# Block-sparse attention and a soft mixture of experts: the dense products joined, the slot input's vector steps moved

## The chip, the cores and the metric

The kernel runs on one core of one Trainium2 chip. A core has five engines with instruction queues of their own: TensorE (PE in the profile; its weight loads are listed apart as PEld), VectorE (DVE), ScalarE (ACT), GpSimd (POOL) and SyncE (SP, which here issues all DMAs). They meet through semaphores. SBUF is the memory that the engines work in, with 128 partitions; PSUM is the memory that PE writes its results to.

The metric is the device time of one execution in microseconds (us), taken as the median of several runs. A profile is one execution with every instruction recorded; its span is the time from the first to the last recorded instruction.

## The reference

Two stages, all in float32. First, block-sparse attention for 4 batches, 8 heads, 768 positions and head size 64, in 24 blocks of 32 positions:

```python
scores = scale * np.matmul(q, k.transpose(0, 1, 3, 2))
mask = np.abs(blk_i - blk_j) <= window          # window = 1: own block and both neighbours
mask = mask | (blk_i == 0) | (blk_j == 0) | (blk_i == n_blocks - 1) | (blk_j == n_blocks - 1)
for qb in range(n_blocks):
    for kb in sampled_blocks[qb]:               # 3 sampled blocks per query block
        mask[qb * block:(qb + 1) * block, kb * block:(kb + 1) * block] = True
scores = np.where(mask, scores, -1000000000.0)
attn = softmax(scores)                          # with 1e-9 added to the sum
out = np.matmul(attn, v)
```

So the first and the last query block see all 24 key blocks ("dense"), the other 22 see at most eight blocks of 32 ("sparse" or "band"). The heads side by side give x with 3072 rows of 512. Second, the mixture:

```python
logits = x @ phi                                # 32 slots: 8 experts with 4 slots each
d = softmax(logits, axis=0)                     # over all 3072 rows
slot_input = d.T @ x                            # 32 x 512
for e in range(8):                              # 4 slots each
    slot_out[e] = np.maximum(slot_input[e] @ w1[e], 0.0) @ w2[e]
c = softmax(logits, axis=1)                     # over the 32 slots
return c @ slot_out
```

w1 and w2 together are 32 MB (8 x 512 x 1024 floats twice).

## The kernel before

**Units.** Attention goes batch by batch. The eight heads are handled at once: four pairs on four groups of 32 partitions, and two halves r of the heads (r = 0, 1). A unit is one softmax step. A dense unit has one half r of the heads and one of the two dense query blocks j, with scores of 128 x 768; four of these make a batch's dense part. A sparse unit has one half r and a pair of neighbouring query blocks (number g of 11), with scores of 128 x 512. `ORDER0` and `ORDER` give the order in which dense (D) and sparse (S) units mix at the start of a batch: DDSSDDSS for the first batch, DSSDDDSS for the others, and then the sparse ones that are left.

**The main loop** (L617 to L677) makes one step n per unit. For each unit it issues, spread over several steps: staging of keys (`stage_k`: POOL and ACT copy the band's keys and the sampled blocks into `kst`, and SP loads queries), staging of gathered values (`stage_v`: POOL, into `vrs`), the scores on PE two units ahead (`do_qk`, into the PSUM tag `s` with 3 buffers), the maximum on DVE and the exponential on ACT (`do_soft`), the transposes of the probabilities on DVE (`do_tr`), and one step later the products with the values on PE. For the band these are `av_half` for a query tile of four query blocks, once per half r (48 and 40 records of one call appear in the timeline as `avt<-vrs` and `avt<-v,ptt`). For the dense blocks it is `av_dense`, once per half r, each with 24 key blocks and two groups g of 64 partitions. All go to `avt`, four PSUM banks in two sets of two, which tiles use in turn. `av_out` divides by the sum and writes x.

**The slot input.** Each finished tile (b, t) of 128 rows of x runs through `moe_front`, six steps e1 to e5: e1 transposes x on PE (`mxt`, in the single PSUM buffer of the tag `pt`) and copies it to `xT` on DVE; e2 makes logits on PE (line L484, into spare columns of `avt`), copied to `lp` by ACT; e3 sums and transposes them on PE (L491, L492, `mlt`, tag `pt` again), and DVE takes a running maximum (`top`, L474 and L477); e3b takes the exponential on ACT (`dT`, L499), a rescaling factor (`al`) and a copy of the logits (`lst`, L504); e4 transposes dT on PE (`md`, L508, tag `pt`), and DVE copies it to `d` (L329) and updates the sum (L512); e5 multiplies d with x on PE (L523, spare columns of `avt`) and DVE adds the result to `sacc` (L526). `EOFF` says in which step after the tile's last unit each of these is issued, and in which of the three lists of a step it stands: lists 0 and 1 at the start of a step (functions that they return run later in the step, after the transposes), list 2 at its end. So the pair (4, 2) is the end of the fourth step. `EOFFL` does the same for one late tile.

**What sets the order.** In the main loop PE and DVE run their instructions in the order in which the program emits them, by hand (`MAN`, manual schedule); after the loop ACT does too. POOL, SP, and ACT in the loop are ordered by the framework's planner, which places an instruction where its estimate finds it ready; a DMA emitted late can therefore stand early in SP's queue.

**Weights.** The 32 MB are loaded in 64 tiles of 512 KB. `NPRE` tiles have space of their own from the start. Two groups go into places that attention has finished with (`EARLYW`: one keys' buffer and the values' buffer v0, issued in the last batch), two more into the other keys' buffer and v1 (`LATEW`), and eleven (`lwb`) into the space of attention's own buffers, behind the loop. What is left goes into tiles that the experts have used up. Then the expert stage and the output follow.

Of the kernel before, what the change touches and what calls it, by code (L numbers as in the profile page):

```python
# [21 lines left out]
P = 128  # L22
# [13 lines left out]
NKST, NVR, NQ, NPTD = 4, 6, 3, 1  # L36
# [9 lines left out]
EOFF = [(2, 2), (4, 1), (4, 2), (4, 2), (5, 1), (6, 2)]  # L46
EOFFL = [(2, 2), (3, 1), (3, 2), (3, 2), (4, 1), (5, 0)]
# [8 lines left out]
NPRE, NLB = 13, 11  # L56
# [10 lines left out]
def attn_moe_kernel(ctx, tc, qT, kT, vtab, sampled, phi, w1, w2, out):  # L67
# [97 lines left out]
    ptd = [pst.tile([P, NB, 2, BLK], F32, name=f"ptd{r}") for r in range(NPTD)]  # L165
# [13 lines left out]
    def load_v(b):  # L179
        vb = vbuf[b % 2].rearrange("p (a f) -> p a f", a=2)  # L180
        if b < 2:
            for p in range(NP):
                POOL.memset(vb[32 * p:32 * p + 32, 1 - p % 2, :], 0.0)  # L183
        for p in range(NP):
            SP.dma_start(out=vb[32 * p:32 * p + 32, p % 2, :], in_=vtab[b, 32 * p:32 * p + 32, :])
        vtile[b] = vb.rearrange("p a (k r d) -> p a k r d", k=NBZ, r=2)
# [145 lines left out]
    def do_tr(u):  # L332
        if u.dense:
            if u.j == 0:
                ptn[0] += 1
            u.pt = ptd[ptn[0] % NPTD]
            for n in range(2):
                DVE.transpose(out=u.pt[:, 12 * n:12 * n + 12, u.j, :], in_=u.p[n])  # L338
        else:
            t, n = (u.g + 1) // 2, 2 * (u.g > 0 and u.g % 2 == 0)  # L340
            if n == 0:
                pts[u.b, t, u.r] = pw.tile([P, 8, 4, BLK], F32, tag="ptt", name="ptt", bufs=PTB)
            u.pt = pts[u.b, t, u.r]
            DVE.transpose(out=u.pt[:, :, n:n + 2, :].rearrange("p k j q -> p j k q"), in_=u.p.rearrange("p j (k q) -> p j k q", k=8))  # L344

    pts = {}
    ptn = [0]

# [14 lines left out]
    def av_out(b, t, av, lo, hi, rs_=slice(0, 2)):  # L363
        n = rs_.stop - rs_.start
        a = av[lo:hi, :, 0:4 * D1].rearrange("p g (r a d) -> p g r a d", r=2, a=2)[:, :, rs_]
        x = new_x(b, t).rearrange("p (g r a d) -> p g r a d", g=2, r=2, a=2)[lo:hi, :, rs_]
# [14 lines left out]
    def av_dense(u):  # L381
        vt = vtile[u.b]
        av = new_set((u.b, "d"), u.r)
        for k in range(NB):
            for g in range(2):
                s_ = slice(64 * g, 64 * g + 64)
                av_mm(av, 64, 64, g, u.r, u.pt[s_, k].rearrange("p j q -> p (j q)"), vt[s_, :, k, u.r, :],
                      k == 0, k == NB - 1)
        return (lambda: av_out(u.b, 0, av, 64, 128)) if u.r else None
# [38 lines left out]
    def moe_front(b, t):  # L428
# [60 lines left out]
        def e3():  # L489
# [3 lines left out]
            top(ps, ps[:, P:P + NS])  # L493
# [12 lines left out]
        def e4():  # L506
            ps = psA.tile([P, NS], F32, tag="pt", bufs=1, name="md")
            PE.transpose(ps, st["dT"][0:NS, :], ident[0:NS, 0:NS])  # L508
            st["d"] = pw.tile([P, NS], F32, tag="d", name="d", bufs=1)
            evac(st["d"], ps, "A" if (b, t) == (B - 1, NT - 2) else "D")  # L510
# [9 lines left out]
        def e5():  # L520
# [4 lines left out]
            if "al" in st:  # L525
                DVE.scalar_tensor_tensor(out=sacc, in0=sacc, scalar=st["al"], in1=ps,  # L526
                                         op0=ALU.mult, op1=ALU.add)
            else:
                DVE.tensor_copy(out=sacc, in_=ps)

        return [f1, f2, f3, e3b, e4, e5] if (b, t) == (B - 1, NT - 1) else [e1, e2, e3, e3b, e4, e5]
# [84 lines left out]
    vn = [0]  # L616
    for n in range(-3, N):  # L617
        if n >= 0:
            pump_k(n + KSTEP)
        while vn[0] < min(N, n + VSTEP + 1):  # L620
# [21 lines left out]
        if n >= 0:  # L642
            t = None
            if u.dense:
                if u.j == 1:
                    at(n + 1, 0, lambda u=u: av_dense(u))
                    t = 0 if u.r == 1 else None
# [12 lines left out]
            if t is not None:  # L660
                if t == 0:
                    both[u.b] = both.get(u.b, 0) + 1
                if n < N - 1 and (t > 0 or both[u.b] == 2):
                    fr = {}
                    for j in range(6):
# [58 lines left out]
    e[5]()  # L724
    c4[3] = c_split(3)
# [41 lines left out]
    load_group(LATEW[0])  # L767
# [205 lines left out]
```

## Time and profile before

| what | value |
|---|---|
| median of 3 runs | 458.24 us (455.7 to 458.44) |
| profiled execution | 453.23 us, of which the span is 451.5 us |
| PE busy | 355.6 us (79%) |
| DVE busy | 241.8 us (54%) |
| ACT busy | 187.4 us (42%) |
| POOL busy | 176.2 us (39%) |
| first dense product starts | 23.9 us |
| attention ends, last weights start to load | about 380 us |
| last weight tiles arrive | about 430 us |

A row of the timeline reads: start in us, duration in us, engine, line of the kernel, operation, out<-in with their shape, number of instructions (x), and in brackets the idle time of the engine just before and what ended it. Shapes such as 64*32 of PE are rows times columns of the array that an instruction uses; a float32 product leaves two records. A row of the table of windows reads: the window, its length, then busy time and instructions of PE, PEld, DVE, ACT and POOL in turn, the clock granted to PE (1.00 is full), the DMA engines' share and their GB/s. A row of a wait reads: who waited, for whom, total us, times, longest.

### The profile page before, as it was taken

How to read it: one execution, taken by the hardware profiler on the slowest of the kernel's cores; microseconds unless marked ns; L12 is line 12 of the kernel's file. 1: busy time of each engine (PE TensorE's matmuls, PEld its weight loads, DVE VectorE, ACT ScalarE, POOL GpSimd, SP SyncE). 2: the span in 40 equal slices, each digit the busy share in tenths (PEclk: the TensorE clock that was granted, in tenths of full speed). 3: DMA queues.
4: the chain of work that ended last, by engine and by line, in shares of the span. 5: the costliest groups of instructions: out<-in, count | busy, mean ns of one | idle time of the engine just before them, and what ended most of it. 6: DMA issues, size and time to landing. Idle time of an engine off the chain costs nothing.

```text
span 451.5 us, 17924 instructions
## 1 busy us (share of the span) xinstructions
PE 355.6 (79%) x7381; PEld 231.5 (51%) x7381; DVE 241.8 (54%) x596; ACT 187.4 (42%) x629; POOL 176.2 (39%) x399
## 2 busy tenths in 40 slices
PE   4688888887978887879788888788878678898760
PEld 0177555555765555547555555566556356344340
DVE  4545566666446665754556666655665854401240
ACT  0524556543235556523455555234554522201340
POOL 9787155654112555532134555321452423300000
PEclk9999999998999999989999999899997888999996
DMA  8565486407001104060010045400000423999998
GB/s 228 111 190 138 139 296 248 149 32 161 13 16 26 28 26 163 28 150 13 25 27 25 18 165 153 155 15 14 26 26 15 140 89 97 383 409 408 406 335 255
DMA packets 26084, 60.31 MB, mean 134 GB/s; under 512 B 2833, under 2 KB 15250, under 8 KB 25490
## 3 DMA queue, kind: packets, MB, share of 16 engines
q1 hardware_dynamic: 26002, 59.16, 40.3%
q8 instruction: 58, 0.95, 0.9%
q14 instruction: 24, 0.20, 0.1%
HBM read 52.86 MB, written 6.29 MB: 131 GB/s over the span
## 4 chain that ended last, share of the span: by engine, by line
PE 42%; DVE 27%; DMA 12%; ACT 9%; issue 5%; ACTq 2%; SPq 0%
PE avt L378 30%; DMA w<-in_w_dram 7%; DVE nm L319 6%; DVE ptt L344 6%; ACT p L322 5%; DVE x L374 4%; PE sd L292 4%; PE mlt L491 2%; DVE ptd L338 2%; ACT kst L218 2%; DMA kw<-in_w_dram 2%; DMA ktile<-in_kT_dram 2%; PE s L303 2%; ACTq L197 1%; DMA out_dram<-ob 1%
## 5 line engine op out<-in xcount | busy, mean ns | idle before, releaser
L229 POOL COPY vrs<-v 128x260 f32 x264 | 97.0, 407 | 131.9 <-PE avt L378 109.0
L378 PE MATMUL avt<-v,ptt 64*64 64x130 f32 (+2 forms) x1728 | 86.8, 300 | 16.5 <-DVE ptt L344 12.2
L218 ACT ACTIVATE kst<-ktile 128x128 f32 x264 | 63.2, 301 | 86.3 <-PE s L303 67.9
L322 ACT ACTIVATE p<-s,nm 128x256 f32<-128x256 f32 x176 | 71.9, 468 | 24.1 <-DVE nm L319 11.7
L378 PEld LDWEIGHTS avt<-v,ptt 64*64 64x64 f32 (+2 forms) x1728 | 57.9, 139 | 46.3 <-DVE ptt L344 22.8
L214 POOL TENSOR_SCALAR kst<-ktile 128x384 f32<-128x384 f32 x88 | 44.1, 513 | 67.3 <-PE s L303 67.3
L303 PE MATMUL s<-kst,qc 64*32 64x256 f32 x1408 | 60.8, 393 | 5.6 <-ACT p L322 4.5
L344 DVE STREAM_TRANSPOSE ptt<-p 128x512 f32<-128x512 f32 x88 | 61.6, 700 | 0.1
L319 DVE TENSOR_REDUCE nm<-s 128x2 f32<-128x512 f32 x88 | 58.4, 663 | 5.7 <-PE s L303 5.6
L378 PE MATMUL avt<-v,ptd 64*64 64x130 f32 x768 | 46.2, 276 | 10.6 <-DVE sacc L526 7.0
L378 PE MATMUL avt<-vrs,ptt 64*32 64x130 f32 x2112 | 51.5, 285 | 0.0
L378 PEld LDWEIGHTS avt<-v,ptd 64*64 64x64 f32 x768 | 44.2, 136 | 12.9 <-DVE sacc L526 7.8
L378 PEld LDWEIGHTS avt<-vrs,ptt 64*32 64x32 f32 x2112 | 41.5, 110 | 0.4
L303 PEld LDWEIGHTS s<-kst,qc 64*32 64x32 f32 x1408 | 24.9, 108 | 25.5 <-ACT p L322 12.2
L292 PE MATMUL sd<-ktile,qd 64*32 64x384 f32 x256 | 31.1, 533 | 8.6 <-DMA ktile<-in_kT_dram 6.5
L316 ACT ACTIVATE pd<-sd,nb 128x384 f32<-128x384 f32 x32 | 16.8, 577 | 47.2 <-DVE nb L313 47.2
L329 DVE COPY d<-md 128x32 f32<-128x32 f32 x23 | 4.4, 192 | 55.9 <-PE md L508 55.9
L310 DVE TENSOR_REDUCE nm<-sd 128x1 f32<-128x384 f32 x32 | 16.7, 544 | 26.1 <-PE sd L292 25.7
L523 PE MATMUL avt<-x,d 128*32 128x128 f32 x192 | 10.2, 284 | 23.5 <-DVE x L374 22.9
L474 DVE TENSOR_REDUCE nmx<-mlt 128x1 f32<-128x128 f32 x24 | 6.9, 289 | 36.4 <-PE mlt L492 35.4
L183 POOL MEMSET v<- 32x3250 f32 x8 | 22.4, 2801 | 0.3
L523 PEld LDWEIGHTS avt<-x,d 128*32 128x32 f32 x192 | 3.8, 107 | 34.7 <-DVE x L374 31.8
(107 smaller groups left out, 352.1 us busy)
## 6 DMA issues: line engine op xcount, KB each, us to landing
w<-in_w_dram SPq DMA_DIRECT2D x37, 512.0 KB, 10.2
v<-in_w_dram SPq DMA_DIRECT2D x18, 512.0 KB, 6.9
v<-in_vtab_dram SPq DMA_DIRECT2D x16, 406.2 KB, 7.8
ktile<-in_kT_dram SPq DMA_DIRECT2D x16, 384.0 KB, 4.5
qc<-in_qT_dram SPq DMA_DIRECT2D x44, 128.0 KB, 2.1
out_dram<-ob SPq DMA_DIRECT2D x20, 256.0 KB, 4.3
kw<-in_w_dram SPq DMA_DIRECT2D x9, 512.0 KB, 5.9
qd<-in_qT_dram SPq DMA_DIRECT2D x4, 128.0 KB, 2.0
```

The source lines that it names most:

```text
L183: POOL.memset(vb[32 * p:32 * p + 32, 1 - p % 2, :], 0.0)
L214: POOL.tensor_scalar(out=st[:, :, w:w + 96], in0=kv[:, :, (i - 1) * BLK:(i + 2) * BLK], scalar1=SCALE, scalar2=1.0, op0=ALU.mult, op1=ALU. ...
L218: ACT.activation(out=st[:, :, o:o + BLK], in_=kv[:, :, ds(vals[j] * BLK, BLK)], func=AF.Copy, scale=SCALE)
L229: POOL.tensor_copy(out=st[:, :, j:j + 1, :], in_=vf[:, :, ds(vals[j], 1), :])
L292: PE.matmul(u.s[n][32 * p:32 * p + 32, :], lhsT=qd[s_, p, u.j, :], rhs=kt[s_, p, 384 * n:384 * (n + 1)], start=True, stop=True)
L303: PE.matmul(u.pair_of[r].s[32 * p:32 * p + 32, j, :], lhsT=q[s_, p, j, :], rhs=kst_[s_, p, :], start=True, stop=True)
L316: ACT.activation(out=u.p[n], in_=u.s[n], func=AF.Exp, bias=nb, scale=SCALE)
L319: DVE.tensor_reduce(out=nm, in_=u.s, axis=AX.X, op=ALU.max, negate=True)
L322: ACT.activation(out=u.p[:, hf, :], in_=u.s[:, hf, :], func=AF.Exp, bias=nm[:, hf:hf + 1], scale=1.0)
L344: DVE.transpose(out=u.pt[:, :, n:n + 2, :].rearrange("p k j q -> p j k q"), in_=u.p.rearrange("p j (k q) -> p j k q", k=8))
L374: DVE.tensor_tensor(out=x, in0=a[:, :, :, 0:D], in1=rs[lo:hi].unsqueeze(3).to_broadcast([hi - lo, 2, 2 * n, D]), op=ALU.mult)
L378: PE.matmul(av[o:o + m, g, r * 2 * D1:(r + 1) * 2 * D1].rearrange("p (a d) -> p a d", a=2), lhsT=lhsT, rhs=rhs, start=start, stop=stop)
```

## The change

- **Dense products.** The two calls of `av_dense` per batch become one, after the fourth dense unit. For each key block it issues both halves r and both groups g, the halves on different columns of the array (output partitions 64 to 127 for r = 0, 0 to 63 for r = 1). There are two buffers `ptd` for the transposed probabilities, one per half, where there was one. The output is divided in two calls of `av_out`, each for one half, and both write rows 64 to 127 of x.
- **Slot input.** The maximum (`top`) and the exponentials (e3b) move from the end of step 4 to the later part of step 5 (`e3t`). The transpose `md` moves from step 5 to the end of step 6 and writes spare columns of `avt` in place of the buffer `pt`. The copy to d and the sum's update (`e4d`) move to the start of step 7, and e5 from the end of step 6 to the start of step 7, with its addition to `sacc` after that step's transposes. One copy that ACT made for one tile is now DVE's like the others.
- **Zeros.** The zeros of the first batch's value buffer were four POOL instructions; two are now DVE's.
- **Weights.** `NPRE` is 12 in place of 13 (the second `ptd` takes the space). The group in the keys' place (`LATEW[0]`) is emitted inside the main loop, as soon as the last unit has been staged, and not behind it.

```diff
-NKST, NVR, NQ, NPTD = 4, 6, 3, 1
+NKST, NVR, NQ = 4, 6, 3
-EOFF = [(2, 2), (4, 1), (4, 2), (4, 2), (5, 1), (6, 2)]
-EOFFL = [(2, 2), (3, 1), (3, 2), (3, 2), (4, 1), (5, 0)]
+EOFF = [(2, 2), (4, 1), (4, 2), (5, 1), (6, 2), (7, 0), (7, 1)]
+EOFFL = [(2, 2), (3, 1), (3, 2), (4, 1), (5, 0), (5, 1), (5, 2)]
-NPRE, NLB = 13, 11
+NPRE, NLB = 12, 11
-    ptd = [pst.tile([P, NB, 2, BLK], F32, name=f"ptd{r}") for r in range(NPTD)]
+    ptd = [pst.tile([P, NB, 2, BLK], F32, name=f"ptd{r}") for r in range(2)]
-                POOL.memset(vb[32 * p:32 * p + 32, 1 - p % 2, :], 0.0)
+                (DVE if b == 0 and p < 2 else POOL).memset(vb[32 * p:32 * p + 32, 1 - p % 2, :], 0.0)
-            u.pt = ptd[ptn[0] % NPTD]
+            u.pt = ptd[u.r]
...
-    def av_dense(u):
-        vt = vtile[u.b]
-        av = new_set((u.b, "d"), u.r)
+    def av_dense(b):
+        vt = vtile[b]
+        av = new_set((b, "d"), 0)
         for k in range(NB):
-            for g in range(2):
-                s_ = slice(64 * g, 64 * g + 64)
-                av_mm(av, 64, 64, g, u.r, u.pt[s_, k].rearrange("p j q -> p (j q)"), vt[s_, :, k, u.r, :],
-                      k == 0, k == NB - 1)
-        return (lambda: av_out(u.b, 0, av, 64, 128)) if u.r else None
+            for r in range(2):
+                for g in range(2):
+                    s_ = slice(64 * g, 64 * g + 64)
+                    av_mm(av, 64 - 64 * r, 64, g, r, ptd[r][s_, k].rearrange("p j q -> p (j q)"), vt[s_, :, k, r, :],
+                          k == 0, k == NB - 1)
+
+        def out():
+            for r in range(2):
+                av_out(b, 0, av, 64 - 64 * r, 128 - 64 * r, slice(r, r + 1), 64)
+        return out
...
-            top(ps, ps[:, P:P + NS])
+            st["mlt"] = ps
+
+        def e3t():
+            def later():
+                top(st["mlt"], st["mlt"][:, P:P + NS])
+                e3b()
+            return later
...
         def e4():
-            ps = psA.tile([P, NS], F32, tag="pt", bufs=1, name="md")
-            PE.transpose(ps, st["dT"][0:NS, :], ident[0:NS, 0:NS])
+            st["md"] = spare(0)[:, 0:NS]
+            PE.transpose(st["md"], st["dT"][0:NS, :], ident[0:NS, 0:NS])
+
+        def e4d():
             st["d"] = pw.tile([P, NS], F32, tag="d", name="d", bufs=1)
-            evac(st["d"], ps, "A" if (b, t) == (B - 1, NT - 2) else "D")
+            evac(st["d"], st["md"], "D")
...
-            if "al" in st:
-                DVE.scalar_tensor_tensor(out=sacc, in0=sacc, scalar=st["al"], in1=ps,
-                                         op0=ALU.mult, op1=ALU.add)
...
+            def later():
+                if "al" in st:
+                    DVE.scalar_tensor_tensor(out=sacc, in0=sacc, scalar=st["al"], in1=ps,
+                                             op0=ALU.mult, op1=ALU.add)
+                else:
+                    DVE.tensor_copy(out=sacc, in_=ps)
+            return later
...
+        if staged[0] == N and LATEW[0] == "ktile" and not latek:
+            latek.append(load_wk(NPRE + sum(KW[tag] for tag in EARLYW), "ktile"))
...
-                if u.j == 1:
-                    at(n + 1, 0, lambda u=u: av_dense(u))
-                    t = 0 if u.r == 1 else None
+                if u.j == 1 and u.r == 1:
+                    at(n + 1, 0, lambda b=u.b: av_dense(b))
+                    t = 0
...
-    load_group(LATEW[0])
+    load_group(LATEW[0], not latek)
```

16 lines of the change are left out of this document (7 added, 9 removed).

## The prediction

> **What bounds the kernel now.** I read the page first: busy shares and the chain that ended last.
>
> ```profile
> span 451.5 us, 17924 instructions
> PE 355.6 (79%) x7381; PEld 231.5 (51%) x7381; DVE 241.8 (54%) x596; ACT 187.4 (42%) x629; POOL 176.2 (39%) x399
> PE 42%; DVE 27%; DMA 12%; ACT 9%; issue 5%; ACTq 2%; SPq 0%
> ```
>
> TensorE (PE) leads, but a quarter of the chain is VectorE (DVE): the two hand work to and fro. Next, the timeline of one period of the band stage (one query tile, four units), engine by engine:
>
> ```profile
> 154.12 1.71 PE L378 MATMUL avt<-v,ptt 64*128 64x130 f32 x40
> 156.73 1.09 PE L303 MATMUL s<-kst,qc 64*32 64x256 f32 x32
> 158.84 0.42 PE L523 MATMUL avt<-x,d 128*32 128x128 f32 x8 [1.02 <-DVE x L374]
> 159.20 0.66 PE L439 MATMUL mxt<-ident,x 128*128 128x128 f32 x4
> 159.79 1.68 PE L303 MATMUL s<-kst,qc 64*32 64x256 f32 x32
> 162.11 1.71 PE L378 MATMUL avt<-v,ptt 64*128 64x130 f32 x40 [0.64 <-DVE ptt L344]
> 165.89 1.71 PE L378 MATMUL avt<-v,ptt 64*128 64x130 f32 x40
> ...
> 154.23 0.29 DVE L474 TENSOR_REDUCE nmx<-mlt 128x1 f32<-128x128 f32 x1 [2.29 <-PE mlt L492]
> 154.55 0.16 DVE L477 TENSOR_TENSOR nmx<-nmx 128x1 f32<-128x1 f32 x1
> 156.84 0.19 DVE L329 COPY d<-md 128x32 f32<-128x32 f32 x1 [2.12 <-PE md L508]
> 157.70 0.13 DVE L372 TENSOR_SCALAR rs<-avt 128x8 f32<-128x8 f32 x1
> 158.71 0.68 DVE L319 TENSOR_REDUCE nm<-s 128x2 f32<-128x512 f32 x1
> 159.31 0.70 DVE L344 STREAM_TRANSPOSE ptt<-p 128x512 f32<-128x512 f32 x1
> 160.75 0.68 DVE L329 COPY xT<-mxt 128x512 f32<-128x512 f32 x1
> ...
> 154.83 0.37 ACT L499 ACTIVATE dT<-mlt,nmx 128x128 f32<-128x128 f32 x1 [1.32 <-DVE nmx L477]
> 155.37 0.17 ACT L504 COPY lst<-mlt 128x32 f32<-128x32 f32 x1
> ```
>
> A period is 165.89 - 154.12 = 11.77 us. DVE stands twice, 2.29 and 2.12 us, in front of a PE result; these are the waits that the change moves. PE's own idle pieces are short and spread out: 1.02 us before L523, a stall inside the scores of 159.79 (1.68 against 1.09 us), and 0.64 us before the first band product. Last, the granted clock, in windows of 3.41 us:
>
> ```profile
> 194.68:198.09 3.41, 1.01 (x12) 0.57 (x12) 3.27 (x10) 0.84 (x2) 2.99 (x9) 1.00 0.97 217
> 198.09:201.50 3.41, 3.18 (x40) 2.72 (x43) 1.40 (x3) 1.05 (x2) 0.00 (x0) 0.50 0.71 146
> 334.62:338.04 3.42, 1.92 (x30) 0.71 (x14) 3.32 (x9) 2.36 (x9) 2.91 (x9) 1.00 0.12 38
> 338.04:341.45 3.41, 2.06 (x32) 0.77 (x32) 3.31 (x9) 2.21 (x9) 2.66 (x6) 0.50 0.02 6
> 157.13:160.54 3.41, 2.39 (x54) 1.03 (x38) 3.34 (x9) 2.26 (x8) 2.87 (x9) 1.00 0.12 38
> ```
>
> The first pair of numbers is PE's busy time and records, the value 1.00 or 0.50 the clock. After a window with 1.01 us of PE work, and after one with 1.92, the whole next window ran at half speed; after 2.39 us it did not. The band stage passes this narrowly.
>
> **The sum, against the profiled execution: 451.5 us of span in 453.23, 5.0 below the median of 458.24.**
>
> *Dense products.* Two products of 96 records become one of 192, whose four 64x64 tiles use all of the array. What four tiles at once cost, against two:
>
> ```profile
> 150.87:151.32 0.45, 0.45 (x18) 0.43 (x16) 1.00 0.65 203
> 217.00:217.45 0.45, 0.45 (x8) 0.45 (x10) 1.00 0.00 0
> ...
> 207.02 1.00 DVE L310 TENSOR_REDUCE nm<-sd 128x1 f32<-128x384 f32 x2
> 208.52 1.05 ACT L316 ACTIVATE pd<-sd,nb 128x384 f32<-128x384 f32 x2 [2.56 <-DVE nb L313]
> 213.20 1.10 PE L303 MATMUL s<-kst,qc 64*32 64x256 f32 x32
> 213.54 1.03 DVE L338 STREAM_TRANSPOSE ptd<-pd 128x384 f32<-128x384 f32 x2
> 216.97 5.57 PE L378 MATMUL avt<-v,ptd 64*64 64x130 f32 x96 [2.32 <-DVE sacc L526]
> ```
>
> In 0.45 us the band's four-tile products (first row) run 16 to 18 records, the dense ones 8 to 10. So the joint product takes about 5.6 us, as long as one half did. What leaves is the first half, which ended just before the scores of 213.20; what was under it comes out. In the new order: the last dense exponentials end at 208.52 + 1.05 = 209.57 and free the score banks; the scores of 213.20 then run 209.6 to 210.7. DVE: its maxima end at 208.0 and two small instructions at 208.4, transposes to 209.4, the slot maximum 0.5, one maximum after the scores to 211.4, transposes 1.0, another maximum 0.6, the copy of d: 213.2. The product runs 213.3 to 218.8 instead of ending at 216.97 + 5.57 = 222.5: 3.7 us. Its output needs six DVE instructions for three: +0.4. From 209.6 to 213.3 PE has only 1.1 us of scores and the small transpose; by the rows above a half-speed window may fall on the product, 1.7 us. So 1.6 to 3.3 gained; I take 2.5, times three batches: **-7.5**.
>
> *Start.* The first batch has the same product before its first band product:
>
> ```profile
> 23.93 7.28 PE L378 MATMUL avt<-v,ptd 64*64 64x130 f32 x96 [2.22 <-DVE ptd L338]
> 31.13 1.49 PE L292 MATMUL sd<-ktile,qd 64*32 64x384 f32 x16
> 24.13 5.78 POOL L229 COPY vrs<-v 128x260 f32 x15 [1.67 <-DVE ptd L338]
> 25.00 0.84 ACT L322 ACTIVATE p<-s,nm 128x256 f32<-128x256 f32 x2
> 4.06 8.48 POOL L183 MEMSET v<- 32x3250 f32 x3
> 4.09 2.82 DVE L142 TENSOR_SCALAR scr<-scr 1x72 f32<-1x72 f32 x1
> ```
>
> The scores of 31.13 can start when ACT frees a bank, 25.84: 5.2 earlier; the gathered blocks (six copies of 0.39 us: 26.4) are in time. With the output's 0.4: **-4.8**, between 0 and -6.2. Zeros on DVE: no DVE memset is in the trace. The 72-element instruction at 4.09 took 2.82 us, exactly one of POOL's memsets beside it, so the two engines seem to take turns; then moving two of them changes nothing, and I take 0. The ends: POOL free two memsets sooner, -5.7 (8.48 / 3 each), if they run side by side and all of it is on the path; +8.6 if DVE pays 4.3 us each (3250 elements at the 1.3 ns of the 512-element maximum of 0.68) and nothing hides it. Both lie far out, since the chain at the start is the load of the keys and not these engines.
>
> *Slot input a step later.* In the new order, from the start of a tile's second band product (+0): PE does that product, then scores, until +3.4. The product is through at about +2.5 (md, 0.17, and the scores follow it at 156.73). DVE, free of its wait, takes rs to x at +2.55 to +3.56 (157.70 to 158.71 lasted 1.01), slot maximum and minimum +0.5, maximum, transpose, maximum and xT at 0.6 each, and only then d: +6.6. ACT's exp, moved behind this maximum, ends by +4.6 and the copy that frees the bank of mxt by +4.9 (0.54 + 0.17 after dT's start). On PE md waits for that exp, mxt behind it for the bank, and L523, now ahead of the next scores, for d: it starts at +6.7, where it started at 158.84 - 154.12 = +4.7. The scores behind it no longer stall (bank free since +5.8), nor does the next product wait for its transpose: it starts at +8.0, as now (162.11 - 154.12). What is late next is the same lp wait. So the period by itself stays 11.8: 0. But PE's idle time is now in one piece: between +3.4 and +6.7 it does md and mxt, 0.9 us, plus the tail of the scores: 1.0 to 1.1 us in 3.4, like the row 194.68. A window of 3.41 us that starts within about 2.0 us of the period's places (from 0.9 before the stretch to 1.1 after it) holds too little; 2.0 / 3.41 = 59% of 12 undisturbed periods = 7. The half-speed window then falls on scores and a band product that PE is the bound of: 1.7 us at most, 0 at least if it falls on the next stall; I take 1.5: **+10.6**. The last batch has half-speed windows already: **+0.5**.
>
> *Weights.* One weight tile less is loaded ahead.
>
> ```profile
> 355.37 1.28 SPq L91 DMA_DIRECT2D kw<-in_w_dram  x3
> SPq L91 <- ACT kst L218: 11.2, 1, 11.2
> 408.56 10.14 DMA kw<-in_w_dram
> ```
>
> The tail is a chain of DMAs: 10.14 us for eight tiles in flight, 1.27 each: **+1.3**. The keys' place is already filled at 355.37, after 11.2 us of waiting for ACT's last key copy; emitting the loads sooner leaves that wait: 0. No query load is queued behind them on SP by then, so an earlier place costs nothing; if their place came later instead, three tiles, 3.8 us.
>
> Sum: -7.5 - 4.8 + 10.6 + 0.5 + 1.3 = +0.1: 453.3, or 458 as a median. **Forecast: 458, no change; its own range 449 to 467.**
>
> **Rivals.** *Faster: the stretch does not cost clock.* For it: PE does work in it, and no single gap in it exceeds 1.3 us. Then -9.9 - 4.8 + 1.3 = -13.4: 445. [...]
>
> *Slower: the periods lock to the windows.* A period lengthened by 1.85 us is 13.65 = 4 x 3.41, so the stretch meets the same place of the window grid each time. Then all 12 periods pay 1.85 (+22.2), and the dense gain is the lower 1.6 (-4.8): -4.8 - 4.8 + 22.2 + 0.5 + 1.3 = +14.4: 473. It decides from about 10 paid periods on. For it: a paying period moves only little against the grid; against: 1.5 us gives 13.3, which drifts 0.4 us per period and leaves.
>
> *The joint product is not faster than two halves* (the tiles of different heads do not overlap): +5.5 in four batches, 480. The row 150.87 speaks against it.
>
> **Chances.** A measurement of this kernel can tell about 1%, 4.6 us, from no change. Forecast 0.52, of which faster by over 1% 0.07, within 0.32, slower 0.13; full clock 0.31, all faster; locked 0.14 and slow product 0.03, all slower. Faster 0.38, same 0.32, slower 0.30. Range 442 to 472: below lies a quarter of the full-clock case (0.08), above half of the locked case and the slow product (0.10).
>
> **What would show it.** The joint product as 192 records in 5.5 to 6 us; L523 starting 6.7 us after the second band product with its wait on d; windows at clock 0.50 in the band stage of the first three batches, where now there are none (7 to 12 forecast); the first band product near 27; the last weight DMAs 1.3 us longer. I am wrong if L523 is not held by d, if the clock stays 1.00 with that stretch, or if the dense stretch does not shorten.

## The result, and the profile after

| | kernel before | changed kernel |
|---|---|---|
| median of four runs | 458.04 us (455.7 to 458.44) | 481.3 us (476.32 to 483.84) |
| ratio | 1 | 1.051 (95% interval 1.042 to 1.061) |
| profiled execution, its span | 453.23 us, 451.5 us | 483.84 us, 482.1 us |

The change makes the kernel 5.1% slower, where no change was forecast, and the time lies outside the range of 442 to 472. The profiled execution is the slowest of the four; the ratio leaves it out, and it was granted 0.850 of the full clock where the other three had 0.854 to 0.884. First the page of the changed kernel: span, busy times, granted clock in forty slices, shares of the chain, and two groups of instructions.

```profile
span 482.1 us, 17948 instructions
PE 374.5 (78%) x7381; PEld 237.2 (49%) x7381; DVE 251.2 (52%) x611; ACT 185.2 (38%) x628; POOL 171.2 (36%) x397
...
PEclk9999988877778888877688898988987885689996
...
PE 52%; DVE 24%; DMA 13%; ACT 4%; issue 3%; SPq 1%; POOL 1%; ACTq 0%; POOLq 0%; DVEq 0%
...
L369 DVE TENSOR_SCALAR rs<-avt 128x8 f32<-128x8 f32 (+3 forms) x33 | 5.4, 163 | 101.9 <-PE avt L375 76.5
...
L375 PE MATMUL avt<-v,ptd 64*64 64x130 f32 x768 | 29.6, 322 | 7.2 <-DVE d L329 6.2
```

The clock row and the dense products' group on the page of the kernel before:

```profile
PEclk9999999998999999989999999899997888999996
...
L378 PE MATMUL avt<-v,ptd 64*64 64x130 f32 x768 | 46.2, 276 | 10.6 <-DVE sacc L526 7.0
```

The 768 records of the dense products are busy for 29.6 us, where they were for 46.2, so the two halves do run side by side. But PE is busy 19 us longer, and its share of the chain rose from 42% to 52% with the same number of records: the same work ran slower. The clock row says why. From the sixth slice to the end of attention it stands mostly below 9. The wait that was to go did not go either: DVE is idle for 101.9 us in front of rs, 76.5 of them on PE (the kernel before had 55.9 us in front of d and 36.4 in front of the maximum).

The timeline of one period shows the new order, PE first, then DVE and ACT:

```profile
166.05 1.71 PE L375 MATMUL avt<-v,ptt 64*128 64x130 f32 x40
...
170.93 0.24 PE L517 MATMUL avt<-ident,dT 32*128 32x32 f32 x1 [1.51 <-ACT dT L508]
...
172.87 0.42 PE L534 MATMUL avt<-x,d 128*32 128x128 f32 x8 [1.03 <-DVE d L329]
...
174.67 2.78 PE L375 MATMUL avt<-v,ptt 64*128 64x130 f32 x40
...
179.55 1.21 PE L375 MATMUL avt<-v,ptt 64*128 64x130 f32 x20
...
168.69 0.17 DVE L369 TENSOR_SCALAR rs<-avt 128x8 f32<-128x8 f32 x1 [4.75 <-PE avt L375]
...
169.74 0.28 DVE L477 TENSOR_REDUCE nmx<-mlt 128x1 f32<-128x128 f32 x1
...
170.42 0.37 ACT L508 ACTIVATE dT<-mlt,nmx 128x128 f32<-128x128 f32 x1 [0.62 <-DVE nmx L480]
```

The slot products (L534) start 172.87 - 166.05 = 6.82 us after the second band product, with their wait on d, as foretold (6.7). In front of them PE waits twice, 1.51 us for the exp that now follows the maximum behind x, and 1.03 for d. DVE's two waits of 2.1 to 2.3 us have become one of 4.75. Then the first band product takes 2.78 us for the forty records that took 1.71. The windows of 3.41 us, in the columns of the prediction, show the reason:

```profile
156.69:160.10 3.41, 1.66 (x29) 1.04 (x37) 3.41 (x8) 2.88 (x11) 3.36 (x10) 1.00 0.15 43
160.10:163.51 3.41, 3.41 (x55) 1.94 (x32) 2.45 (x6) 2.28 (x9) 2.08 (x5) 0.50 0.12 38
170.34:173.75 3.41, 1.78 (x37) 1.12 (x45) 3.41 (x8) 2.88 (x11) 3.41 (x10) 1.00 0.12 38
173.75:177.17 3.42, 3.42 (x63) 2.04 (x55) 2.59 (x5) 2.54 (x10) 1.64 (x4) 0.50 0.14 43
184.00:187.41 3.41, 1.94 (x39) 1.20 (x45) 3.41 (x8) 2.80 (x11) 3.41 (x11) 1.00 0.12 35
187.41:190.82 3.41, 3.41 (x64) 2.23 (x56) 2.61 (x5) 2.84 (x10) 2.18 (x6) 0.50 0.52 163
```

A window with 1.66 to 1.94 us of PE work, then one at half clock, and again exactly 13.65 us later: four windows. The period, 11.77 us before, is now 179.55 - 166.05 = 13.50, close to 13.65, so the thin stretch meets nearly the same place of the grid each time. That is the second rival's picture. From the first batch's bands up to the last batch's, 28 windows ran at half clock, where three did before. Fourteen of them lie in the bands of the first three batches, where none did before and the prediction priced seven.

Where the 30.6 us of span came from, by the starts of the band products of tiles 1 and 5 in each batch: the four tiles of the bands, 8.4, 8.5 and 6.9 longer in the first three batches and 3.8 in the last; the three dense stretches between them, +1.8, +1.5 and -2.6; start +0.2; from the start of the last band product to the end +2.0.

The start. POOL's timeline, PE's, and two rows of DVE at the very beginning, a zero fill and the copy behind it:

```profile
22.93 5.64 POOL L183 MEMSET v<- 32x3250 f32 x2
28.63 5.91 POOL L229 COPY vrs<-v 128x260 f32 x15
...
29.08 0.65 PE L375 MATMUL avt<-vrs,ptt 64*32 64x130 f32 x4 [0.55 <-POOL vrs L229]
...
40.05 5.57 PE L375 MATMUL avt<-v,ptd 64*64 64x130 f32 x188 [0.64 <-DVE ptd L336]
...
1.47 2.77 DVE L183 MEMSET v<- 32x3250 f32 x1 [1.47 <-PEq L977]
4.27 2.82 DVE L133 COPY sreg<-scr 1x72 int32<-1x72 int32 x1
```

In this first batch the joint product has its 5.57 us for 188 records at full clock; in the other three it took 8.33, 8.37 and 6.92 us, at half clock in whole or in part. But two fills of the second batch's values (22.93) now stand in front of the gathered copies, which began at 24.13 before and at 28.63 now, and the first band product waits for them.

### The profile page after: what moved, and what is told of

Read it like the earlier page. It is cut to its first block, busy times and chain, and to the rows that moved or that the text cites. A ratio compares the mean times of both kernels' runs of the same rounds, so it can differ in the third digit from the quotient of the medians.

```text
span 482.1 us, 17948 instructions
## 1 busy us (share of the span) xinstructions
PE 374.5 (78%) x7381; PEld 237.2 (49%) x7381; DVE 251.2 (52%) x611; ACT 185.2 (38%) x628; POOL 171.2 (36%) x397
## 4 chain that ended last, share of the span: by engine, by line
PE 52%; DVE 24%; DMA 13%; ACT 4%; issue 3%; SPq 1%; POOL 1%; ACTq 0%; POOLq 0%; DVEq 0%
PE avt L375 33%; DMA w<-in_w_dram 8%; PE s L303 8%; DVE nm L319 5%; PE sd L292 4%; DVE x L371 4%; DVE ptt L342 3%; DVE xT L329 3%; PE avt L534 2%; DMA v<-in_w_dram 2%; DMA ktile<-in_kT_dram 2%; PE mlt L494 2%; PE avt L487 2%; DVE nm L310 1%; DVE rs L370 1%
## 5 line engine op out<-in xcount | busy, mean ns | idle before, releaser
L375 PE MATMUL avt<-v,ptt 64*64 64x130 f32 (+2 forms) x1728 | 102.9, 336 | 3.9 <-DVE d L329 3.2
L375 PEld LDWEIGHTS avt<-v,ptt 64*64 64x64 f32 (+2 forms) x1728 | 69.2, 161 | 43.7 <-issue 22.2
L322 ACT ACTIVATE p<-s,nm 128x256 f32<-128x256 f32 x176 | 71.7, 468 | 13.5 <-DVE nm L319 7.4
L303 PE MATMUL s<-kst,qc 64*32 64x256 f32 x1408 | 66.6, 454 | 6.9 <-ACT pd L316 3.9
L369 DVE TENSOR_SCALAR rs<-avt 128x8 f32<-128x8 f32 (+3 forms) x33 | 5.4, 163 | 101.9 <-PE avt L375 76.5
L375 PE MATMUL avt<-vrs,ptt 64*32 64x130 f32 x2112 | 56.4, 298 | 1.1 <-POOL vrs L229 1.1
L292 PE MATMUL sd<-ktile,qd 64*32 64x384 f32 x256 | 37.7, 642 | 10.2 <-DMA ktile<-in_kT_dram 6.0
L375 PE MATMUL avt<-v,ptd 64*64 64x130 f32 x768 | 29.6, 322 | 7.2 <-DVE d L329 6.2
L375 PEld LDWEIGHTS avt<-v,ptd 64*64 64x64 f32 x768 | 28.4, 165 | 8.3 <-DVE d L329 6.6
L517 PE MATMUL avt<-ident,dT 32*128 32x32 f32 x24 | 6.0, 252 | 32.7 <-ACT dT L508 32.3
L534 PE MATMUL avt<-x,d 128*32 128x128 f32 x192 | 12.2, 332 | 19.5 <-DVE d L329 17.7
L292 PEld LDWEIGHTS sd<-ktile,qd 64*32 64x32 f32 x256 | 10.4, 128 | 26.8 <-issue 14.4
```

Of the source, the lines that this page charges most:

```text
L292: PE.matmul(u.s[n][32 * p:32 * p + 32, :], lhsT=qd[s_, p, u.j, :], rhs=kt[s_, p, 384 * n:384 * (n + 1)], start=True, stop=True)
L303: PE.matmul(u.pair_of[r].s[32 * p:32 * p + 32, j, :], lhsT=q[s_, p, j, :], rhs=kst_[s_, p, :], start=True, stop=True)
L322: ACT.activation(out=u.p[:, hf, :], in_=u.s[:, hf, :], func=AF.Exp, bias=nm[:, hf:hf + 1], scale=1.0)
L375: PE.matmul(av[o:o + m, g, r * 2 * D1:(r + 1) * 2 * D1].rearrange("p (a d) -> p a d", a=2), lhsT=lhsT, rhs=rhs, start=start, stop=stop)
L534: PE.matmul(ps[32 * c:32 * c + 32, :], lhsT=st["d"], rhs=x[:, c * P:(c + 1) * P], start=True, stop=True)
```

## The experiments

Theory after the result: the slot input's new order puts maximum, exp, md, d and slot products into one chain behind x; PE then has too little work in one window of each period, the next window is at half clock, and the period locks to four windows. Rivals: the new order's chain is longer by itself and the clock only follows; or the joint product brings the half clock. Ratios below are to the kernel before, which was measured again beside each set of runs (medians of 453.1 to 455.0 us), with 95% intervals.

### Which part makes the loss

```diff
 dense_alone: the kernel before, and only
-    def av_dense(u):
+    def av_dense(b):        # both halves; two ptd; NPRE 12
```

> The kernel before with the joint dense product, two transposed buffers, and one weight tile less; the slot input keeps its old order, all zeros are POOL's. Theory 1 (the late slot input makes the loss, through the clock): 458 - 7.5 (dense) - 4.8 (start, since POOL's order is the old one) + 1.3 = 447; no half-clock windows in the band stage of the first three batches; joint products of 5.6 us; band stages of 47.7 us per four tiles. Rival (the joint product or its longer wait brings the half clock by itself): 460 or more, with half-clock windows beside each joint product.

Measured 454.04 us, 0.997 (0.993 to 1.001), between the two expectations. The loss is not there, but of the gain only 3.2 us at the start are (the second band product of tile 1 stands at 50.95 us, where it stood at 54.20). The bands are clean, 47.6 to 48.4 us per four tiles. Its dense stretch is not:

```profile
195.06:198.48 3.42, 1.38 (x18) 0.94 (x20) 3.32 (x9) 1.30 (x4) 2.39 (x7) 1.00 0.96 205
198.48:201.89 3.41, 3.41 (x49) 2.82 (x49) 0.80 (x2) 0.50 (x2) 0.00 (x0) 0.50 0.56 115
205.30:208.72 3.42, 2.24 (x28) 0.93 (x20) 2.63 (x9) 0.56 (x3) 1.79 (x5) 1.00 0.12 37
```

With the first half's product gone from the middle of the stretch, PE has little to do before the joint one (2.24 us in the window at 205.30), the clock falls a second time at 208.72, and the product is paid at half speed, 7.3 to 7.6 us in three batches where the first batch has 5.6. The time from a batch's last band product to the next batch's first is 37.2 to 39.3 us (36.7 to 36.9 before).

```diff
 slot_alone: the kernel before, and only the new EOFF, EOFFL, e3t, md in spare columns, e4d, e5's later addition
```

> The kernel before with the slot input's new order alone; dense products, zeros and weights as before. Theory 1: periods of 13.3 to 13.65 us, some 20 half-clock windows 13.65 us apart, band stages of about 56 us per four tiles; 458 + 3 x 8 + 4 = about 485. Rival (the dense change makes the loss): 455 to 462.

Measured 479.08 us, 1.052 (1.044 to 1.061): the whole loss. Its second band products:

```profile
150.50 1.71 PE L378 MATMUL avt<-v,ptt 64*128 64x130 f32 x40
...
162.52 1.71 PE L378 MATMUL avt<-v,ptt 64*128 64x130 f32 x40
...
176.01 1.71 PE L378 MATMUL avt<-v,ptt 64*128 64x130 f32 x40
```

An undisturbed period of the new order takes 12.02 us, 0.25 longer than the old one; the next, with a half-clock window, 13.49. There are 14 such windows up to the last batch, not 20, as the first period of each batch, in the first batch the first two, stays clean. Four tiles of the bands take 54.7 to 54.9 us in the first three batches, where they took 47.5 to 48.0.

### Is it the clock?

The sharpest test adds work and should make the kernel faster.

```diff
 fill: the changed kernel, and in e1 behind the transposes and in e4 ahead of md
+            for c in range(6):
+                PE.transpose(spare(1)[:, 0:120], ident[0:120, :], ident[0:120, 0:120])
```

> The changed kernel with twelve added TensorE transposes per tile whose results nothing reads, six ahead of md and six behind mxt, 2 us of work in two waits that last 1.5 and 1.0 us. Theory 1 (the clock is the loss): the thin windows fill up, few half-clock windows are left in the band stage of the first three batches, four tiles take 47 to 50 us again; 458 to 465, though work was added. Rival (the new order's own chain of DVE, ACT and TensorE is longer, and the clock only follows): periods stay at 13.3 to 13.7 us; 480 to 490.

Measured 446.97 us, 0.984 (0.977 to 0.992): 34 us less than the changed kernel, with 282 transposes more, and better than forecast. The page's clock row; then one period and a joint product in the timeline; then the window that holds the gap:

```profile
PEclk9997999999999999999999999999998699999896
```

```profile
153.19 1.71 PE L375 MATMUL avt<-v,ptt 64*128 64x130 f32 x40
...
157.01 0.84 PE L519 MATMUL avt<-ident 120*128 120x120 f32 x6 [0.46 <-DVE x L371]
...
160.00 0.42 PE L538 MATMUL avt<-x,d 128*32 128x128 f32 x8 [0.41 <-DVE d L329]
...
165.27 0.99 PE L375 MATMUL avt<-v,ptt 64*128 64x130 f32 x12
...
211.08 5.58 PE L375 MATMUL avt<-v,ptd 64*64 64x130 f32 x192 [1.50 <-DVE d L329]
```

```profile
155.63:159.04 3.41, 2.72 (x49) 1.90 (x32) 3.11 (x8) 1.91 (x10) 2.40 (x7) 1.00 0.19 43
```

The slot products still wait for d and start 6.81 us after the second band product; the chain is the same. But no window between 45 us and the last batch is at half clock, the period shown is 12.08, and the joint product takes 5.6 us in every batch. So the clock carries most of the loss. The rival that blames the chain keeps a part: with the clock at full, four tiles still take 49.6 to 50.7 us, 7.3 us more over the first three batches than in the kernel before, of the 23.8 in the changed kernel; the added work's own cost is in these 7.3. From a batch's last band product to the next one's first it is now 31.4 to 31.5 us, 5.2 to 5.4 less than before.

```diff
 fill_half: fill with range(2) in both places
```

> The changed kernel with four added transposes per tile instead of twelve, two ahead of md and two behind mxt (0.55 us). [...] Rival (any work in the gap is enough, a gap's length decides): none left, 447.

Measured 468.69 us, 1.034 (1.031 to 1.037), with 17 half-clock windows up to the last batch, where the changed kernel has 28; the rival, 447 us with no such window left, missed. A third of the work gives back about a third of what fill does (12.6 of 34.3 us), so here it was not enough that something interrupts the gap; how much PE did there counted.

```diff
 before_fill: the kernel before, with fill's twelve transposes per tile
```

> The kernel before with the same twelve added transposes per tile, results unread. It tells how much of the gain of the filled changed kernel belongs to the added work alone. Theory: the kernel before has few half-clock windows (one before each dense stretch, five in the last batch), so they end, 3 x 1.8 + 4 = about -9, and the added work costs up to 0.4 us per period in places where it does not fall into a wait: 447 to 455. Rival (the added work brings all of the gain, and the change nothing): 445 or less, as fast as the filled changed kernel.

Measured 497.28 us, 1.095 (1.088 to 1.101). Both expectations missed, for a reason of the experiment's own:

```profile
161.92 0.84 PE L428 MATMUL avt<-ident 120*128 120x120 f32 x6 [1.03 <-DVE sacc L532]
```

In the old order the addition to sacc stands right behind the slot products, and the transposes, which write to the accumulators' banks, wait for it (21.6 us in 18 places) and hold the scores behind them; the period rises to 14.65. It says nothing of what fill tests. A second version writes to md's bank, in front of the slot products:

```diff
 before_fill2: the kernel before
+            fill(st["mdp"], P, 7)      # in e5, ahead of the slot products
```

> The kernel before with seven added transposes per tile, results unread, in front of the slot products and into a bank of their own, so that they wait for nothing that the slot products do not wait for later; 0.95 us of work in a wait of 1.02. It tells what the half-clock windows of the kernel before cost. Theory: the windows before the dense stretches (three) go, those of the last batch in part: 453 - 5 = 445 to 450. Rival (the first filled version of this kernel was slow because added work as such costs time): 465 or more.

Measured 454.19 us, 0.997 (0.993 to 1.002), against 445 to 450 expected. Up to the end of attention it still has seven half-clock windows, where the kernel before has eight; that PE's other gaps there lie where nothing was added is likely, and not shown. But it shows that such work in a wait is free (in the second and third batch four tiles take 48.0 and 47.6 us, as before), and that fill's gain is not the added work's alone.

### Which half of the slot input's move

```diff
 e5_later
-EOFF = [(2, 2), (4, 1), (4, 2), (5, 1), (6, 2), (7, 0), (7, 1)]
+EOFF = [(2, 2), (4, 1), (4, 2), (5, 1), (6, 2), (7, 0), (7, 2)]
```

> The changed kernel with the slot products (wait on d) put behind the next scores instead of ahead of them; nothing else. Theory 1: the scores start 1 us sooner and share the stretch, which holds 1.6 us of work more evenly; the lock is lost or halved: 462 to 475. Rival (order in DVE decides, not the place on TensorE): 478 to 485.

Measured 480.01 us, 1.054 (1.046 to 1.063). The theory's expectation missed: where the slot products stand on PE does not matter, with 23 half-clock windows up to the last batch. The wait of md for the exp is unmoved, 1.51 us. But the windows now mostly come in pairs, and not 13.65 us apart: in the second batch the periods are 12.56, 15.09, 12.81 and 17.37 us. So the loss does not need the lock to one place of the grid, only the thin stretch.

```diff
 d_late
-EOFF = [(2, 2), (4, 1), (4, 2), (5, 1), (6, 2), (7, 0), (7, 1)]
+EOFF = [(2, 2), (4, 1), (4, 2), (4, 2), (5, 1), (6, 0), (6, 2)]
```

> The changed kernel with only the half of the slot input's move that concerns d: the slot maximum and the exp stand where they stood in the kernel before, md too; d is copied behind x, and the slot products follow the scores. Theory (the lock comes from putting maximum, exp, md, d and the slot products behind x in one chain, so that TensorE has 1 us of work in 3.4): md and its scores are back in their old place, the chain behind x is only d: no half-clock windows spaced 13.65 in the first three batches, 445 to 458. Rival (any later d starves TensorE): 475 or more.

```diff
 max_late
-EOFF = [(2, 2), (4, 1), (4, 2), (5, 1), (6, 2), (7, 0), (7, 1)]
+EOFF = [(2, 2), (4, 1), (4, 2), (5, 1), (6, 1), (6, 1), (6, 2)]
```

> The changed kernel with only the other half: the slot maximum behind x as in the change, md and d as soon after it as they can, the slot products a step earlier than in the change. Theory: maximum, exp, md and d still make one chain behind x, and TensorE waits for it: 470 to 485, with windows 13.65 apart. Rival (the late d is what locks): 445 to 460.

Measured: d_late 443.64 us, 0.969 (0.957 to 0.981), 1.4 us below the range expected; max_late 471.86 us, 1.036 (1.022 to 1.049). So one half of the move gains and the other loses. One period of d_late in the timeline, PE and then DVE:

```profile
150.34 1.71 PE L375 MATMUL avt<-v,ptt 64*128 64x130 f32 x40
...
152.77 0.24 PE L517 MATMUL avt<-ident,dT 32*128 32x32 f32 x1
...
154.98 0.43 PE L534 MATMUL avt<-x,d 128*32 128x128 f32 x8 [0.94 <-DVE d L329]
...
161.81 1.71 PE L375 MATMUL avt<-v,ptt 64*128 64x130 f32 x40
...
150.45 0.29 DVE L477 TENSOR_REDUCE nmx<-mlt 128x1 f32<-128x128 f32 x1 [2.18 <-PE mlt L495]
...
153.06 0.17 DVE L369 TENSOR_SCALAR rs<-avt 128x8 f32<-128x8 f32 x1 [1.50 <-PE avt L517]
```

md follows the band product with no wait, because the maximum stands early and the exp is long done. DVE still waits 2.18 us for the maximum, but only 1.50 before rs, where it waited 2.12 for md before. The period is 161.81 - 150.34 = 11.47, the next 11.23. No window of the bands is at half clock up to the last batch. max_late keeps the wait of 1.51 us for the exp, and has 23 half-clock windows up to the last batch.

```diff
 before_d_late: the kernel before, with slot_alone's edits and d_late's EOFF
```

> The kernel before with only d copied behind x and the slot products' result added later; dense products, zeros and weights as before. Theory (the wait of VectorE for md, 2.12 us, is worth some 0.4 us of each period, and nothing else moves): bands of 45.8 us per four tiles instead of 47.6, no lock: 454 - 4 x 1.8 = 447. Rival (the gain of the version with the late d came from the joint product): 452 to 456.

Measured 443.93 us, 0.976 (0.969 to 0.983), 3 us below the estimate: the late d alone is worth about 11 us. In the profiled executions it gains 5.8 us in the bands of all four batches, near the 7 of the estimate, and 5.2 in the three dense stretches, which the estimate left out; 2.2 are lost behind the last band product, which ran at half clock. From a batch's last band product to the next batch's first it takes 34.0, 35.5 and 35.5 us; d_late_pz (below), which has the joint product, takes 33.5, 35.8 and 35.6. So the joint product adds nothing there, as in dense_alone.

### The dense term

```diff
 dense_fill: dense_alone, with transposes into the accumulators' spare columns ahead of the slot
 products of tile 4, behind mxt and ahead of md of tile 5, ahead of the joint product, and in the last batch
```

> The joint dense product with the old slot order, and added transposes only where this kernel's trace shows half-clock windows: ahead of the slot products of tile 4, behind mxt and ahead of md of tile 5, ahead of the joint product, and in the last batch. Theory (the old order keeps the bands at 11.8 us per tile, and the joint product gains what was forecast once the clock stays): joint product 5.6 us, from a batch's last band product to the next batch's first some 31.5 to 33 us instead of 37.4, three times: 454 - 15 - 4 = 435 to 440. Rival (the joint product starts too late in the old order to gain): 447 or more.

Measured 463.83 us, 1.027 (1.021 to 1.033). The same fault as in before_fill: added work in the accumulators' banks waits for DVE (18.4 us in 15 places) and holds what follows, and three of the joint products are still partly at half clock (7.2 to 7.9 us). The time is in the rival's range, but with this fault nothing follows for the theory.

```diff
 dense_fill2: dense_alone, and seven transposes ahead of each slot product (md's bank);
 for tile 5 ten ahead of md (mlt's bank) and ten behind the slot products (md's bank)
```

> The joint dense product with the old slot order, with seven added transposes in front of the slot products of every tile, and ten ahead of md and ten behind the slot products of tile 5, all into banks that do not wait for VectorE's reads of the accumulators. Theory (the joint product gains when the clock stays): joint product 5.6 us, 32 to 33 us from a batch's last band product to the next batch's first instead of 37.4: 454 - 15 = 437 to 442. Rival (the joint product starts too late in the old order to gain): 448 or more.

Measured 451.75 us, 0.991 (0.986 to 0.996). The joint product takes 5.58 us in all batches, as expected, but the stretch is 35.5 to 36.7 us, not 32 to 33. It starts 25 to 26.2 us after the last band product; in fill it is 20.3. The time is the rival's, and so is the reason: in the old order of tile 5's slot input the joint product comes too late, and ten transposes ahead of md waited 2.63 us for ACT's copy and then held md. The last of these kernels has the work where nothing waits for it, in the better order (and all zeros on POOL, below):

```diff
 d_late_fill: d_late_pz, and
+            if t == 5 and b < B - 1:
+                fill(spare(1), 0, 12)                      # ahead of md
+            if t in (4, 5) and b < B - 1:
+                fill(spare(0), 0, 8 if t == 4 else 6)      # behind the slot products
```

> The same with 26 added transposes per batch, results unread, in the three gaps of the dense stretch: eight behind the slot products of tile 4, twelve ahead of md and six behind the slot products of tile 5. Theory (the joint product, 7.6 us there, is still paid at half clock): joint product 5.6 us and 32 to 33 us from a batch's last band product to the next batch's first instead of 35.7: 440 - 8 = 430 to 434. Rival (the added work delays the joint product by as much as the clock gives back): 438 to 441.

Measured 429.04 us, 0.943 (0.936 to 0.949), the fastest version: 26 us below the kernel before measured beside it (455.00) and 10 below d_late_pz. In the second batch:

```profile
184.93 1.04 PE L431 MATMUL avt<-ident 120*128 120x120 f32 x8
...
194.70 1.43 PE L431 MATMUL avt<-ident 120*128 120x120 f32 x12
...
199.79 0.83 PE L431 MATMUL avt<-ident 120*128 120x120 f32 x6
201.33 7.23 PE L375 MATMUL avt<-v,ptd 64*64 64x130 f32 x192 [0.71 <-DVE sacc L547]
```

The stretch is 34.2, 33.0 and 34.7 us, where d_late_pz has 33.5, 35.8 and 35.6; that is 3.0 of the 5.3 us between the two profiled executions. Five half-clock windows are left up to the last batch, where d_late_pz has ten, and three in the last batch instead of six. The joint product itself still meets one or two (7.2 to 7.9 us), so of the theory's numbers the time came, and the stretch nearly, but not the joint product of 5.6; part of the rest came in the last batch, where nothing was edited, and its cause stays open.

### The start

```diff
 fill_pool_zeros: fill, and
-                (DVE if b == 0 and p < 2 else POOL).memset(...)
+                POOL.memset(...)
```

> The filled changed kernel with all zeros on POOL as in the kernel before. Theory for the start (taking two zero fills off POOL made the planner put two fills of the second batch ahead of the gathered copies, which hold the first band product): copies start near 23 to 24 us instead of 28.6, the first tile's second band product near 51 instead of 55.2: 447 - 4 = 443. Rival (POOL's zeros hold the start, as the change supposes): 447 to 450.

```diff
 d_late_pz: d_late, with the same edit
```

> The changed kernel with d alone late, and all zeros on POOL. Theory (the moved zeros cost the start, by the planner's place for the second batch's zeros): first tile's second band product near 50 us instead of 54.8: 443.6 - 4 = 439 to 440. Rival (the start is set by something else and the 5 us are lost again in the first batch): 443 to 445.

Measured: fill_pool_zeros 444.43 us, 0.982 (0.976 to 0.988), near the 443 expected; d_late_pz 439.21 us, 0.967 (0.961 to 0.973), 4.4 below d_late, as expected. POOL in d_late_pz:

```profile
24.71 5.78 POOL L229 COPY vrs<-v 128x260 f32 x15 [1.67 <-DVE ptd L336]
30.55 5.64 POOL L183 MEMSET v<- 32x3250 f32 x2
```

The second batch's zeros stand behind the copies again, and the second band product of tile 1 starts at 50.20 us, where it was 54.82 in d_late. In fill_pool_zeros it is 49.55 against 55.21; there a half-clock window in the first batch takes back part of the gain.

## Why the prediction was wrong, step by step

Between the forecast sum of +0.1 and the measured +30.6 us of span lie 13.2 from the slot input, 8.3 from the dense products, 5.0 from the start, 3.3 from the last batch and 0.7 from the weights.

- **Slot input, +10.6.** This is the largest step that failed, by its size: the bands of the first three batches cost +23.8. The mechanism stood in it: a stretch with little PE work, the half-clock window after it, and the slot products 6.7 us after the second band product (6.82 measured). But it took the stretch's places on the window grid as independent of each other, paid in 59% of 12 periods, seven windows. Eleven periods paid, with fourteen windows. They are not independent: a period that pays once lasts 13.2 to 13.5 us and meets the grid at nearly the same place, as the lock rival says, and I gave that 0.14. My argument against it, that 13.3 us would drift away by 0.4 us per period, fails by the prediction's own numbers: at 0.4 a period it takes five periods to cross the 2.0 us of places that I counted as too thin, and a batch has four. The periods of 13.38 to 13.52 us drift by 0.13 to 0.27. That the rival's 22.2 comes so close to 23.8 is in part luck: eight periods paid 1.4 to 1.75 us and not 1.85, one paid nothing, and the last of each batch, with two half-clock windows, paid 3.35 to 3.8. The stretch was also a little fuller than estimated (1.66 to 1.94 us in the windows shown against 1.0 to 1.1), and that did not save the clock.
- **"The period by itself stays 11.8."** Without a half-clock window it is 12.02 to 12.08 us in slot_alone and fill: wrong by 0.25 to 0.3, about 3 us over twelve periods. In fill the last period of each batch is longer by more, 13.4 to 14.1 us where it was 12.3; how much of that the added work costs is not shown.
- **Last batch, +0.5.** +3.8. Ten windows there ran at half clock instead of five, seven of them before the start of the last band product, up to which the 3.8 is counted.
- **Dense products, -7.5.** The rate was right (5.57 us for 188 records, 5.6 at full clock throughout fill), and the rival of a slow product fell. What failed is the price of the clock. The prediction allowed for at most one half-clock window in each of the three stretches, 1.7 us; six, six and two ran there in the changed kernel, and the stretches together gave +0.8. With the clock kept, fill gained 5.2 to 5.4 in each, more than the 3.3 of the prediction's upper end; part of it is the half-clock window that the kernel before has there.
- **Start, -4.8.** +0.2. The term itself exists: with all zeros on POOL the second band product of tile 1 comes 3.2 to 4.7 us earlier than in the kernel before (50.95 in dense_alone, 50.20 in d_late_pz and 49.55 in fill_pool_zeros, against 54.20). The step that failed is "moving two of them changes nothing": it priced the zeros on the engines and not the planner, which put the next batch's zeros into POOL's freed time, ahead of the copies that the first band product needs. DVE's zeros took 2.77 us each, below the 4.3 taken as the upper end.
- **Weights, +1.3.** Where the last band product ran at full clock, from its start to the end it took 72.6 to 73.0 us with 13 tiles ahead (the kernel before, before_fill, before_fill2) and 73.9 to 74.7 with 12 (fill, fill_half, fill_pool_zeros, dense_fill, dense_fill2): +0.9 to +2.1, which holds the forecast. In the changed kernel it is +2.0, in which the last product's half clock (4.21 against 2.43 us) stands too.
- **The rival of full clock.** It fell, 0.31 was too much. It counted on work in the stretch and on gaps of no more than 1.3 us; but the three windows of the changed kernel shown above that were followed by half speed had 1.66 to 1.94 us of work, and in the one at 170.34 no wait of PE was longer than 1.51 us. The row of 334.62 in the prediction already spoke against it: 1.92 us of work, and half clock at 338.04. The half-clock windows shown lie on one grid: 13.65 us or four windows apart in the changed kernel, and 139.95 us or 41 windows apart in the kernel before (198.09 and 338.04).

The halves of one edit had opposite signs, and the prediction priced them together. Moving d behind x alone takes away DVE's wait for md and gains 11 us (before_d_late). Moving the maximum behind x puts ACT's exp and md into the path between x and the slot products, and PE pays for it (1.51 us for the exp, and 471.86 us, in max_late).

## What to carry to other kernels

When a tuned loop is rearranged, read its work per clock window, not only its waits: here a step that gathered PE's idle pieces into one stretch (1.66 to 1.94 us of work in the windows shown) made the bands of three batches 23.8 us longer, and with a period of 13.50 us, near four windows of 3.41, the half clock came again and again. Test this by adding useless work to the gap: in fill, 282 transposes more made the kernel 34 us faster, and so showed the clock as the cost. Put that work into a bank that nothing else waits for: before_fill, which did not, took 497.28 us; before_fill2, with seven transposes per tile in md's bank, 454.19. Try the parts of a move one at a time (d_late 443.64 us, max_late 471.86), and look where the planner puts other work into the time that a move frees (here the gathered copies began 4.5 us later).

## What the runs showed of the hardware

No single busy time separates the windows of these runs that half clock followed from the others. Here are windows of dense_alone, and after them one of slot_alone and one of the kernel before:

```profile
287.22:290.64 3.42, 3.42 (x45) 2.93 (x50) 1.15 (x2) 0.84 (x2) 0.00 (x0) 0.50 0.08 29
290.64:294.05 3.41, 3.41 (x67) 2.31 (x54) 2.25 (x6) 0.71 (x2) 0.34 (x1) 1.00 0.00 0
294.05:297.46 3.41, 2.56 (x34) 1.09 (x28) 2.46 (x9) 0.61 (x2) 1.85 (x6) 1.00 0.03 7
297.46:300.88 3.42, 1.65 (x33) 0.84 (x33) 1.57 (x6) 1.85 (x7) 0.07 (x1) 0.50 0.00 0
```

```profile
70.57:73.98 3.41, 1.85 (x49) 1.14 (x36) 2.96 (x8) 1.01 (x5) 2.31 (x8) 1.00 1.02 404
...
126.41:129.82 3.41, 1.48 (x26) 1.48 (x28) 2.50 (x6) 2.28 (x7) 0.04 (x1) 1.00 0.12 41
```

2.56 us of busy time, two windows after a half-clock one, were followed by half speed; 1.85 us after a long stretch at full clock were not (the next window, with 2.40 us, ran at 1.00). The kernel before shows the same, and the prediction left these rows out: 1.48 us at 126.41, and 1.60 and 1.70 us in its like at 215.16 and 303.90, were not followed by half speed, though 1.92 us at 334.62 were. Fuller windows ahead do not explain that, since the window ahead of 126.41 had 3.02 us and the one ahead of 334.62 had 3.41. So the busy time of the records is not by itself what the clock goes by, and the prediction's reading of a bound between 1.92 and 2.39 us does not hold. What it goes by stays open.

A zero fill of 32 x 3250 floats took 2.77 us on DVE beside POOL's fill and 2.77 alone, so the fills did not slow each other, and the prediction's "seem to take turns" does not hold for them. It fits the small instructions: the DVE copy of 72 numbers at 4.27, 0.03 us after the start of a POOL fill, took 2.82 us and ended 0.05 us behind that fill, as the instruction of 72 numbers at 4.09 did in the kernel before.
